# Values one step later, the closing steps reordered, and spare matmuls in TensorE's gaps, in a decode kernel that streams its caches

## The chip, the cores and the metric

One core of a Trainium2 chip. The metric is device microseconds of one execution. The times below are from executions in the fast state, timed in rounds beside the kernel before on the same chip; only the single look at the kernel before (the last row of the table of experiments) has an unknown state. A profiled execution also has a span, from the first to the last instruction; it is some 1.8 us shorter than the device time (211.0 and 212.79 us for the changed kernel). In this kernel TensorE multiplies matrices into tiles of the memory PSUM, VectorE and ScalarE work on them, and DMA engines move the loads (87.32 MB, 87.17 of them through one queue). The views of the profile call TensorE PE (its loading of weights PEld), VectorE DVE, ScalarE ACT and GpSimd POOL.

## The reference, cut to what matters

A decode step of batch 4 with one new token: the sum of the input, an attention branch and an MLP branch. Only the last W = 2048 positions of the caches are read. The arrays are bfloat16.

```python
q = (xn @ wq)                                   # 32 query heads, 16 K/V heads, Dh = 128
scores = einsum(q, k_cache[:, :, -2048:]) * Dh ** -0.5
o = einsum(softmax(scores), v_cache[:, :, -2048:]) @ wo
h = gelu(layernorm(x1) @ w3) @ w4               # 576 -> 4608 -> 576
out = x + o + (x1 + h)
```

With one token, the shifted parts of the MLP's first half are zeros and drop out. What is left is reading 87 MB: 16 K tiles and 16 V tiles of 2 MB each, wq, wo, w3 and w4.

## The kernel before

One queue issues all loads. K and V tiles share a ring of six buffers; the seventh tile waits until the first has been used. The weights w4 come last, in six pieces, so that little work is left when the last bytes land.

```python
    W4_PIECES = [0, NFH, NF - 12, NF - 6, NF - 2, NF - 1, NF]      # rows 0-18-24-30-34-35-36
    order = [("K", 0), ("K", 1), ("K", 2)]
    for h in range(Hkv):
        order.append(("V", h))
        if h + 3 < Hkv:
            order.append(("K", h + 3))
    # ... w3 after V2, wo in four parts ahead of V0, V4, V8, V12, w4 at the end
```

A step t computes the scores of head t, the softmax of head t-1, the values of head t-2 and the output of head t-3. Each step has four slices.

```python
    for t in range(Hkv):
        hm, hv, hf, hp = t - 1, t - 2, t - 3, t - 4
        for s in range(NSL):
            # ... K transpose of the next slice on VectorE; softmax pieces of head hm
            if hv >= 0:
                pv(hv, s)            # O += P^T V, 4 matmuls
            k_scores(t, s)           # 4 matmuls of 512 columns
            # ... output of head hf: o_scale (ScalarE), o_turn (TensorE), o_sum (VectorE)
```

Then come the closing steps.

```python
    sm_max(hl); sm_rec(hl - 1); o_scale(hl - 2)          # hl = 15
    pv(hl - 1, 0); sm_maxT(hl); sm_neg(hl); pv(hl - 1, 1)
    sm_sub(hl); sm_exp(hl); o_turn(hl - 2)
    pv(hl - 1, 2); pv(hl - 1, 3); o_sum(hl - 2)
    sm_turn(hl); sm_den(hl); sm_rec(hl); o_scale(hl - 1)
    for s in range(NSL):
        pv(hl, s)
    o_scale(hl); o_turn(hl - 1); o_sum(hl - 1)
    o_turn(hl); o_sum(hl); o_spread(hl); o_pick(hl)
    mlp_out(*pieces[0])              # 18 rows of w4, sums in acc and acc_odd in turn
    o_proj(hl)                       # the last 16 matmuls with wo
    mlp_out(*pieces[1])
    mlp_out(*pieces[2])
    mlp_out(*pieces[3])
    # ... copy acc_odd to SBUF (ScalarE), pieces 4 and 5 into acc, one add (VectorE), store
```

(Several statements are put on a line here; the kernel has one on each.)

## Time and profile before

| | before |
|---|---|
| device time, median of 3 (range) | 211.53 us (211.49 to 211.63) |
| span of the profiled execution | 209.8 us |
| moved by DMA | 87.32 MB, mean 416 GB/s |
| TensorE waiting for V tiles | 37.1 us |
| first matmul of w4's piece 0 | 201.13 us |
| first matmul of piece 3 | 206.04 us |
| start of the last add | 207.26 us |

From the page of the kernel before, the DMA rows of the span in 40 slices (busy share in tenths, then GB/s):

```profile
DMA  7999999999999999999999999999999999999991
GB/s 301 400 412 437 428 428 428 436 422 428 469 408 420 433 428 427 438 431 428 431 437 428 422 425 446 425 425 436 422 436 428 421 435 440 425 425 448 418 402 72
```

The table of windows of the kernel before. Its columns are the stretch and its length in us, the busy time and instruction count of each engine (PE, PEld, DVE, ACT, POOL), the TensorE clock that was granted (1.00 is full), the busy share of the DMA engines and GB/s:

```profile
126.00:170.00 44.00, 37.23 (x231) 15.68 (x230) 34.02 (x54) 6.88 (x15) 0.00 (x0) 0.96 1.01 431
206.00:206.50 0.50, 0.46 (x8) 0.37 (x8) 0.00 (x0) 0.00 (x0) 0.00 (x0) 1.00 0.26 90
206.50:207.00 0.50, 0.50 (x8) 0.26 (x3) 0.00 (x0) 0.26 (x1) 0.00 (x0) 1.00 0.00 0
```

The loads run without a hole from the first slices to 206.5 us, so they bound this kernel. The mean of 126 to 170 us is 431 GB/s. (Single slices read above that, up to 469, so only the longer means are used here.)

The waits of TensorE for tiles in the kernel before, and VectorE's for K (total us, times, longest us):

```profile
PE O L390 <- DMA vn<-in_A_v_cache_dram: 37.1, 10, 14.0
PE S L338 <- DVE kt L225: 3.1, 1, 3.1
DVE kt L225 <- DMA kn<-in_A_k_cache_dram: 10.6, 1, 10.6
```

TensorE waits for values ten times: compute is ahead of the loads. The end of its timeline before (start, length, engine, line, operation, how many, and in brackets the idle time before it with what ended it), single lines of it:

```profile
201.13 0.29 PE L183 MATMUL acc<-w_sb,gT 128*8 128x288 bf16 x1
205.66 0.29 PE L183 MATMUL acc<-w_sb,gT 128*8 128x288 bf16 x1
206.04 0.28 PE L183 MATMUL acc<-w_sb,gT 128*8 128x288 bf16 x1
207.26 0.45 DVE L613 TENSOR_TENSOR fin<-acc,odd 8x288 bf16<-8x288 f32 x1
```

TensorE works from 201.13 to 205.95 without a gap. It begins piece 3 at 206.04, and the chain of waits says that this was the landing of w4. So TensorE arrives just ahead of the last pieces, by 0.1 to 0.3 us.

### The profile page before, as it was taken

What the parts mean: (1) busy time and instruction counts of PE and PEld (TensorE: products, weight loads), DVE (VectorE), ACT (ScalarE), POOL (GpSimd) and SP (SyncE); (2) the same over time, 40 slices, a digit from 0 to 9 for tenths busy, and PEclk for the clock granted to TensorE, in tenths of its full rate; (3) what the DMA queues carried; (4) which work ended last, traced back from release to release, by engine and by line L of the source; (5) the groups of instructions that cost most, each with busy time, mean ns of one, the idle gap of its engine ahead of it and who ended that gap; (6) DMA issues with size and microseconds to landing.
All of it is one profiled execution on the core that took longest, in us unless ns stands there. A gap on an engine that the chain in (4) does not pass through costs nothing.

```text
span 209.8 us, 2403 instructions
## 1 busy us (share of the span) xinstructions
PE 149.9 (71%) x955; PEld 62.8 (30%) x955; DVE 120.4 (57%) x217; ACT 33.9 (16%) x64; POOL 2.8 (1%) x15
## 2 busy tenths in 40 slices
PE   0287496869694009659899599977994926989884
PEld 0133132223231003214364143332532401425362
DVE  3741899584831082816706869995299471771421
ACT  7602201020211000202102121120111110202300
POOL 4010000000000000000000000000000000000000
PEclk9999589696969556958999979997999985969999
DMA  7999999999999999999999999999999999999991
GB/s 301 400 412 437 428 428 428 436 422 428 469 408 420 433 428 427 438 431 428 431 437 428 422 425 446 425 425 436 422 436 428 421 435 440 425 425 448 418 402 72
DMA packets 6659, 87.32 MB, mean 416 GB/s; under 512 B 748, under 2 KB 1016, under 8 KB 1656
## 3 DMA queue, kind: packets, MB, share of 16 engines
q1 hardware_dynamic: 6640, 87.17, 97.5%
q8 instruction: 7, 0.11, 0.2%
q14 instruction: 4, 0.03, 0.0%
q10 hardware_dynamic: 8, 0.00, 0.0%
HBM read 87.17 MB, written 0.00 MB: 415 GB/s over the span
## 4 chain that ended last, share of the span: by engine, by line
DMA 72%; PE 18%; DVE 6%; ACT 1%; issue 1%; SPq 0%; DVEq 0%
DMA vn<-in_A_v_cache_dram 35%; DMA w_sb<-in_B_w_dram 31%; PE S L338 7%; DMA wq_sb<-in_A_wq_dram 6%; DVE kt L225 3%; PE acc L183 2%; PE g_ps L456 2%; PE q_ps L285 2%; PE O L390 2%; PE oT L403 1%; DVE qz L317 1%; PE gT_ps L468 1%; DVE mx L344 1%; PE S L360 1%; ACT q_sb L296 1%
## 5 line engine op out<-in xcount | busy, mean ns | idle before, releaser
L225 DVE STREAM_TRANSPOSE kt<-kn 128x1024 int32<-128x1024 int32 x64 | 76.4, 1217 | 10.9 <-DMA kn<-in_A_k_cache_dram 10.6
L338 PE MATMUL S<-kt,qz 128*128 128x512 bf16 x256 | 79.7, 441 | 3.1 <-DVE kt L225 3.1
L390 PE MATMUL O<-vn,PT 128*32 128x512 bf16 x256 | 27.4, 426 | 38.9 <-DMA vn<-in_A_v_cache_dram 37.1
L338 PEld LDWEIGHTS <-qz 128*128 128x128 bf16 x256 | 21.7, 104 | 41.5 <-issue 25.8
L366 ACT ACTIVATE E<-S 128x512 bf16<-128x512 f32 x16 | 9.5, 597 | 122.6 <-PE S L360 122.6
L390 PEld LDWEIGHTS <-PT 128*32 128x32 bf16 x256 | 7.2, 94 | 47.3 <-issue 30.2
L372 DVE STREAM_TRANSPOSE PT<-E 128x512 bf16<-128x512 bf16 x16 | 11.4, 710 | 14.9 <-ACT E L366 14.9
L356 DVE TENSOR_REDUCE nm<-mg 8x1 bf16<-8x16 f32 x16 | 2.4, 152 | 20.7 <-PE mg L351 20.7
L397 ACT ACTIVATE O_sb<-O,rd 128x512 f32<-128x512 f32 x16 | 11.0, 686 | 15.6 <-issue 11.0
L413 DVE TENSOR_REDUCE on<-oT 128x8 bf16<-128x128 f32 x16 | 4.5, 280 | 12.7 <-PE oT L403 12.7
L403 PE MATMUL oT<-ident_w,O_sb 128*128 128x128 f32 x64 | 11.1, 302 | 0.3 <-ACT O_sb L397 0.3
L344 DVE TENSOR_REDUCE mx<-S 128x1 f32<-128x512 f32 x16 | 10.5, 657 | 1.3 <-PE S L338 1.3
L403 PEld LDWEIGHTS oT<-ident_w,O_sb 128*128 128x128 f32 x64 | 9.2, 161 | 5.3 <-issue 2.9
L183 PE MATMUL acc<-wo_sb,op 128*8 128x288 bf16 x56 | 7.5, 286 | 0.0
L376 PEld LDWEIGHTS dn<-rs,same_j 128*128 128x128 f32 x32 | 5.8, 188 | 2.9 <-ACT E L366 0.7
L360 PE MATMUL S<-nm,j_row 8*128 8x512 bf16 x16 | 6.5, 409 | 0.0
L329 PE MATMUL S<-negbig,ohT 4*128 4x512 bf16 x16 | 6.2, 385 | 0.0
L351 PE MATMUL mg<-dm,sel_jb 128*8 128x16 bf16 x16 | 2.8, 175 | 3.7 <-DVE dm L346 3.5
L183 PEld LDWEIGHTS <-op 128*8 128x8 bf16 x64 | 4.7, 87 | 2.2 <-issue 0.5
L351 PEld LDWEIGHTS <-sel_jb 128*8 128x8 bf16 x16 | 1.3, 83 | 13.1 <-DVE dm L346 6.5
L183 PE MATMUL acc<-w_sb,gT 128*8 128x288 bf16 x38 | 5.2, 286 | 0.1
L474 DVE COPY g_x<-gT_ps 128x64 f32<-128x64 f32 (+1 forms) x3 | 0.6, 195 | 7.7 <-PE gT_ps L468 7.7
(93 smaller groups left out, 84.3 us busy)
## 6 DMA issues: line engine op xcount, KB each, us to landing
kn<-in_A_k_cache_dram SPq DMA_DIRECT2D x16, 2048.0 KB, 21.9
vn<-in_A_v_cache_dram SPq DMA_DIRECT2D x16, 2048.0 KB, 24.4
wo_sb<-in_A_wo_dram SPq DMA_DIRECT2D x4, 1152.0 KB, 24.5
w_sb<-in_B_w_dram SPq DMA_DIRECT2D x1, 4608.0 KB, 34.3
wq_sb<-in_A_wq_dram SPq DMA_DIRECT2D x1, 4096.0 KB, 12.8
w_sb<-in_B_w_dram SPq DMA_DIRECT2D x1, 2592.0 KB, 31.9
w_sb<-in_B_w_dram SPq DMA_DIRECT2D x2, 864.0 KB, 33.9
w_sb<-in_B_w_dram SPq DMA_DIRECT2D x2, 576.0 KB, 33.0
```

What stands on the lines that cost most here:

```text
L183: nc.tensor.matmul(out=to[q:q + OR, :], lhsT=lhsT[:, NI - 1 - i:NI - 1 - i + OR], rhs=rhs[:, i * CW:(i + 1) * CW], start=start, stop=False ...
L225: nc.vector.transpose(out=kt[:], in_=src)
L329: nc.tensor.matmul(out=S_ps[h][:].rearrange("p (c k) -> p c k", k=QD), lhsT=ohT[:], rhs=negbig[:].unsqueeze(1).to_broadcast([B, SC, QD]), ...
L338: nc.tensor.matmul(out=S_ps[h][:], lhsT=qz[:, z0:z0 + P], rhs=kt[:, ib, :, e:2 * QD:2].rearrange("p c k -> p (c k)"), start=False, stop=Fa ...
L344: nc.vector.reduce_max(out=mx[:], in_=S_ps[h][:], axis=AX.X)
L360: nc.tensor.matmul(out=S_ps[h][:], lhsT=j_row[:], rhs=st.pop(("nm", h))[:, 0:1].to_broadcast([NJ, NW]), start=False, stop=False, skip_grou ...
L366: nc.scalar.activation(out=E[h][:].rearrange("p c k -> p (c k)"), in_=S_ps.pop(h)[:], func=ACT.Exp, scale=scale, accum_out=rs[:])
L372: nc.vector.transpose(out=PT[h][:], in_=E.pop(h)[:])
L376: nc.tensor.matmul(out=dn[:], lhsT=same_j[:], rhs=st.pop(("rs", h))[:], start=True, stop=True)
L390: nc.tensor.matmul(out=O_ps[h][g * QD:(g + 1) * QD], lhsT=PT[h][:, c, :], rhs=vn[:, :, c, :], start=(s == 0), stop=False, skip_group_check ...
L397: nc.scalar.activation(out=O_sb[h][:], in_=O_ps.pop(h)[:], func=ACT.Copy, scale=st.pop(("rd", h))[:, 0:1])
L403: nc.tensor.transpose(out=oT[:, s, :], in_=o[:, s, :], identity=ident_w[:, s * NJ:s * NJ + P])
```

## The change

The intent: with values three steps behind the scores, a step no longer starts with a wait for the V tile that has only just been asked for, and in the closing less is left to do when V15 lands. The output of head 15 now goes through the projection before piece 0. Where TensorE would stand idle, it multiplies into a spare PSUM tile that nobody reads, in order to hold its clock up (in the kernel before it was 0.50 from 184.76 to 188.17 us, after 3.41 us in which TensorE was busy for 1.86 us). The diff, cut:

```diff
-        E[h] = ptp.tile([P, SC, QD], BF16, tag="e", name="E")
+        E[h] = ptp.tile([P, SC, QD], BF16, tag="e", name="E", bufs=1)
-        PT[h] = ptp.tile([P, SC, QD], BF16, tag="pt", name="PT")
+        PT[h] = ptp.tile([P, SC, QD], BF16, tag="pt", name="PT", bufs=3)
...
-    G_AT = 7
+    G_AT = 9                                    # the step that also runs the MLP's w3
-        hm, hv, hf, hp = t - 1, t - 2, t - 3, t - 4
+        hm, hr, hv, hf, hp = t - 1, t - 2, t - 3, t - 4, t - 5
...
+    def keep_warm(n):
+        if not warm:
+            warm.append(ps_s.tile([P, NW], F32, tag="S", name="warm"))
+        for _ in range(n):
+            nc.tensor.matmul(out=warm[0][0:OR, :], lhsT=ln2T[:, 0, 0:OR], rhs=qz[:, 0:NW], start=True, stop=True)
...                                              # head 15's softmax among the values of head 13
+    for s in range(NSL):
+        pv(hl - 1, s)
+    o_turn(hl - 2)
+    o_sum(hl - 2)
     o_scale(hl - 1)
+    o_turn(hl - 1)
+    o_sum(hl - 1)
+    keep_warm(6)
     for s in range(NSL):
         pv(hl, s)
     o_scale(hl)
-    o_turn(hl - 1)
-    o_sum(hl - 1)
...
+    keep_warm(2)
     o_turn(hl)
     o_sum(hl)
+    keep_warm(2)
     o_spread(hl)
     o_pick(hl)
+    keep_warm(4)
+    o_proj(hl)
+    keep_warm(3)
+    pieces = list(zip(W4_PIECES, W4_PIECES[1:]))
     mlp_out(*pieces[0])
-    o_proj(hl)
     mlp_out(*pieces[1])
+    keep_warm(3)
     mlp_out(*pieces[2])
+    keep_warm(1)
     mlp_out(*pieces[3])
```

The spare matmuls fall in three groups, which the text below calls the six (ahead of the values of head 15), the eight (2, 2 and 4, each behind a step that waits for ScalarE or VectorE) and the seven (3, 3 and 1, around the pieces of w4).

More of the change, by code (lines that the diff above doesn't have):

```diff
@@ L527 @@
                     sm_max(hm)
-                if hv >= 0:
-                    sm_rec(hv)
+                if hr >= 0:
+                    sm_rec(hr)
                 if hp >= 0:
@@ L567 @@
         flush_loads()
+    acc_odd = ps_acc.tile([P, CW], F32, tag="g", name="acc_odd")
+    second += [acc_odd, True]
+    warm = []
+    def keep_warm(n):
[3 more added lines that the diff above has]
+            nc.tensor.matmul(out=warm[0][0:OR, :], lhsT=ln2T[:, 0, 0:OR], rhs=qz[:, 0:NW], start=True, stop=True)
     hl = Hkv - 1
@@ L571 @@
     sm_rec(hl - 1)
-    o_scale(hl - 2)
-    pv(hl - 1, 0)
+    o_pick(hl - 4)
+    o_scale(hl - 3)
+    pv(hl - 2, 0)
     sm_maxT(hl)
     sm_neg(hl)
-    pv(hl - 1, 1)
+    pv(hl - 2, 1)
+    o_turn(hl - 3)
     sm_sub(hl)
     sm_exp(hl)
-    o_turn(hl - 2)
-    pv(hl - 1, 2)
-    pv(hl - 1, 3)
-    o_sum(hl - 2)
+    pv(hl - 2, 2)
+    pv(hl - 2, 3)
+    o_sum(hl - 3)
     sm_turn(hl)
+    o_proj(hl - 4)
     sm_den(hl)
     sm_rec(hl)
+    o_scale(hl - 2)
+    for s in range(NSL):
+        pv(hl - 1, s)
+    o_turn(hl - 2)
+    o_sum(hl - 2)
     o_scale(hl - 1)
+    o_turn(hl - 1)
+    o_sum(hl - 1)
+    keep_warm(6)
     for s in range(NSL):
@@ L589 @@
     o_scale(hl)
-    o_turn(hl - 1)
-    o_sum(hl - 1)
-    pieces = list(zip(W4_PIECES, W4_PIECES[1:]))
-    acc_odd = ps_acc.tile([P, CW], F32, tag="g", name="acc_odd")
-    second += [acc_odd, True]
+    keep_warm(2)
     o_turn(hl)
     o_sum(hl)
+    keep_warm(2)
     o_spread(hl)
     o_pick(hl)
+    keep_warm(4)
+    o_proj(hl)
+    keep_warm(3)
+    pieces = list(zip(W4_PIECES, W4_PIECES[1:]))
     mlp_out(*pieces[0])
-    o_proj(hl)
     mlp_out(*pieces[1])
+    keep_warm(3)
     mlp_out(*pieces[2])
+    keep_warm(1)
     mlp_out(*pieces[3])
```

## The prediction

> **What bounds it now.** Loads. The table of windows shows 426 to 432 GB/s and a DMA share of 0.99 to 1.01 in every stretch from 6 to 190 us: the loads never starve. 87.3 MB at about 430 GB/s is 203 us of the 209.8 us span. [...] The chain of waits gives 72% to DMA; TensorE waits 37.1 us for values. Compute is ahead: a step costs TensorE and VectorE 8 to 9 us, a K and V pair about 9.7 us of DMA.
>
> **The end, before** (timeline). Piece 0 of w4 lands at about 200.5 us (168.6 + 31.9). TensorE runs without a gap from 201.13 (piece 0, attention projection, pieces 1, 2) to 205.67, then waits 0.29 us for piece 3, landed at 206.00. The last piece lands at about 206.8 (issue 184.6 + 22.2). Then 0.4 us ACT copy, 0.14 + 0.45 us DVE, store. TensorE already waits for DMA at the end.
>
> **What the change does.**
> - Values one step later. V was loaded right after the K of its step and stalled TensorE at each step's start; now the step waits for K only. The waits move to the K transposes on DVE; nothing is removed.
> - A value buffer is freed one step later, so V(h) is issued with K(h+3), not a step earlier. By my estimate from landing times, 9 to 14 us of loads are still queued then, even in the MLP step (about 4 us longer). No starvation expected. Buffers of wo and w3 also come free later, still ahead of need.
> - Closing: less attention work remains when V15 lands (estimate 194.3 us: V13 at 184.65 and 4.8 us per tile). Traced durations: PV 1.05, scale 0.7, turn 0.66, sum 0.3, spread 0.35, pick 0.85, projection 0.95, gaps: done at about 199.5, before piece 0 lands. TensorE gains some 1.5 to 2 us of slack.
> - 21 spare matmuls of 512 columns, about 0.22 us each at the granted clock of 1.00 after 190 us (four scores take 1.07 us with weight loads): 4.6 us. Six stand before V15, eight in waits on ACT/DVE; the other seven eat the slack. Piece 2 then runs to about 205.7, before piece 3 lands. [...] this trace has the clock at 1.00 in every window from 190 us on: nothing to win.
>
> **On the critical path:** nothing up to piece 3's landing; after it the same few matmuls, copy, add and store. The gain is at most 0.3 us; the loss as small, unless the spare matmuls run slow.
>
> **Predicted:** 211.4 us, 8 in 10 between 210.7 and 212.1. Faster by over 2%: 0.01; within 2%: 0.98; slower by over 2%: 0.01.
>
> **What would show it.** DMA as full as before, 415 GB/s overall; last piece of w4 landing within 0.5 us of 206.8; TensorE's waits for vn nearly gone, DVE's for kn grown to 30 us or more; the last V tiles issued about 10 us later; TensorE idle (or in spare matmuls) before pieces 0 to 3; clock 1.0 at the end, same distance from last landing to end.
>
> **What would make it wrong.** A bubble in the loads after the w3 load or the MLP step, because value buffers come free late (up to a few us); spare matmuls at half clock delaying piece 3 (up to 1 us); the last w4 packets spread differently over the 16 engines (in the last 1.5 us only part of them works), 0.3 us either way.

## The result

| | before | after |
|---|---|---|
| device time, median of 6 (range) | 211.59 us (211.49 to 211.89) | 212.96 us (212.68 to 213.23) |
| ratio, 95% interval | | 1.0062 (1.0048 to 1.0075) |
| span of the profiled execution | 209.8 us | 211.0 us |
| start of the last add | 207.26 us | 208.43 us |

A ratio is the mean time of one kernel's fast runs over that of the other's in the same rounds, so it is not quite the ratio of the medians quoted beside it. The change costs 1.3 us. That is within 2%, but outside the range predicted. The last add starts 1.17 us later, which is the whole difference of the spans.

The same rows of the page after, and the same windows with two more at the end:

```profile
DMA  7999999999998999999999999999999999999990
GB/s 299 398 432 432 429 419 435 430 425 438 489 419 380 445 422 408 449 432 429 432 429 435 425 421 436 441 421 432 436 422 425 430 436 444 404 441 441 404 370 18
```

```profile
126.00:170.00 44.00, 36.41 (x219) 15.66 (x215) 31.56 (x53) 6.78 (x15) 0.00 (x0) 0.92 1.01 431
206.00:206.50 0.50, 0.50 (x9) 0.26 (x6) 0.00 (x0) 0.00 (x0) 0.00 (x0) 1.00 0.21 74
206.50:207.00 0.50, 0.50 (x11) 0.35 (x7) 0.00 (x0) 0.00 (x0) 0.00 (x0) 1.00 0.00 0
207.00:207.50 0.50, 0.50 (x10) 0.29 (x6) 0.00 (x0) 0.00 (x0) 0.00 (x0) 1.00 0.00 0
207.50:208.00 0.50, 0.50 (x8) 0.36 (x5) 0.00 (x0) 0.07 (x1) 0.00 (x0) 1.00 0.00 0
```

The loads are as full as before and end in the same window, 206.0 to 206.5. No time was lost there, although buffers come free a step later. The difference is that TensorE is now still busy after them: in 207.0 to 208.0 it has 1.00 us of work. The waits of TensorE after, and the wait of VectorE to which those for values have moved:

```profile
PE S L338 <- DVE kt L225: 31.3, 10, 14.3
```

```profile
DVE kt L225 <- DMA kn<-in_A_k_cache_dram: 36.7, 10, 15.0
```

There is no wait for V any more. As predicted, the waiting has moved from V to K: TensorE's waits for V go from 37.1 us to none, its waits for K's transposes from 3.1 us to 31.3, and VectorE's waits for K itself from 10.6 us to 36.7. In sum none of it is gone: TensorE was idle for 59.9 us of the span before; after, it was idle for 56.7 us and in spare matmuls for about 4.5 us (21 of 0.215; the six of them at 195.43 us took 1.29 us). The end of the timeline after, single lines of it:

```profile
192.96 1.05 PE L390 MATMUL O<-vn,PT 128*32 128x512 bf16 x16
194.85 0.66 PE L403 MATMUL oT<-ident_w,O_sb 128*128 128x128 f32 x4 [0.26 <-ACT O_sb L397]
195.43 1.03 PE L577 MATMUL warm<-qz,ln2T 128*8 128x512 bf16 x4
196.53 1.23 PE L390 MATMUL O<-vn,PT 128*32 128x512 bf16 x10
197.59 0.59 PE L577 MATMUL warm<-qz,ln2T 128*8 128x512 bf16 x2
201.06 0.29 PE L183 MATMUL acc<-wo_sb,op 128*8 128x288 bf16 x1
202.26 0.38 PE L577 MATMUL warm<-qz,ln2T 128*8 128x512 bf16 x1
202.47 0.38 PE L577 MATMUL warm<-qz,ln2T 128*8 128x512 bf16 x1
208.43 0.43 DVE L635 TENSOR_TENSOR fin<-acc,odd 8x288 bf16<-8x288 f32 x1
```

From 201.06 on, not one gap of TensorE is left: it never waits for w4. A spare matmul shows as 0.38 us long, but the next starts 0.21 us after it (202.26, 202.47), and that spacing is what it costs. The values of head 15 are held behind the six, and piece 3 is begun at 207.2 us, when the loads have ended.

### The profile page after: what moved, and what is told of

Its sections match the earlier page's. It is cut to its first block, busy times and chain, and to the rows that moved or that the text cites. A ratio compares the mean times of both kernels' runs of the same rounds, so it can differ in the third digit from the quotient of the medians.

```text
span 211.0 us, 2418 instructions
## 1 busy us (share of the span) xinstructions
PE 154.3 (73%) x976; PEld 64.6 (31%) x976; DVE 120.2 (57%) x217; ACT 33.8 (16%) x64; POOL 2.7 (1%) x15
## 4 chain that ended last, share of the span: by engine, by line
DMA 63%; PE 24%; DVE 5%; issue 3%; SPq 2%; ACT 1%; DVEq 0%; ACTq 0%
DMA kn<-in_A_k_cache_dram 63%; PE S L338 8%; PE acc L183 4%; PE O L390 4%; DVE kt L225 3%; PE oT L403 2%; PE g_ps L456 2%; PE warm L577 2%; DVE mx L344 1%; SPq L103 1%; PE S L360 1%; ACT O_sb L397 1%; PE gT_ps L468 1%; DVE dm L346 1%; PE mg L351 0%
## 5 line engine op out<-in xcount | busy, mean ns | idle before, releaser
L338 PE MATMUL S<-kt,qz 128*128 128x512 bf16 x256 | 78.8, 437 | 31.4 <-DVE kt L225 31.3
L225 DVE STREAM_TRANSPOSE kt<-kn 128x1024 int32<-128x1024 int32 x64 | 76.6, 1222 | 37.0 <-DMA kn<-in_A_k_cache_dram 36.7
L338 PEld LDWEIGHTS <-qz 128*128 128x128 bf16 x256 | 22.6, 104 | 69.6 <-issue 53.5
L403 PE MATMUL oT<-ident_w,O_sb 128*128 128x128 f32 x64 | 12.0, 320 | 0.7 <-ACT O_sb L397 0.7
L360 PE MATMUL S<-nm,j_row 8*128 8x512 bf16 x16 | 7.0, 439 | 0.1
L183 PE MATMUL acc<-wo_sb,op 128*8 128x288 bf16 x48 | 6.5, 286 | 0.0
L577 PE MATMUL warm<-qz,ln2T 128*8 128x512 bf16 x21 | 5.7, 379 | 0.0
L183 PE MATMUL acc_odd<-w_sb,gT 128*8 128x288 bf16 x34 | 5.3, 286 | 0.0
L285 PE MATMUL q_ps<-wq_sb,xnT 128*32 128x512 bf16 x40 | 4.1, 594 | 0.9 <-DMA wq_sb<-in_A_wq_dram 0.9
```

Source lines behind the costliest of these rows:

```text
L183: nc.tensor.matmul(out=to[q:q + OR, :], lhsT=lhsT[:, NI - 1 - i:NI - 1 - i + OR], rhs=rhs[:, i * CW:(i + 1) * CW], start=start, stop=False ...
L225: nc.vector.transpose(out=kt[:], in_=src)
L338: nc.tensor.matmul(out=S_ps[h][:], lhsT=qz[:, z0:z0 + P], rhs=kt[:, ib, :, e:2 * QD:2].rearrange("p c k -> p (c k)"), start=False, stop=Fa ...
L360: nc.tensor.matmul(out=S_ps[h][:], lhsT=j_row[:], rhs=st.pop(("nm", h))[:, 0:1].to_broadcast([NJ, NW]), start=False, stop=False, skip_grou ...
L403: nc.tensor.transpose(out=oT[:, s, :], in_=o[:, s, :], identity=ident_w[:, s * NJ:s * NJ + P])
L577: nc.tensor.matmul(out=warm[0][0:OR, :], lhsT=ln2T[:, 0, 0:OR], rhs=qz[:, 0:NW], start=True, stop=True)
```

## The experiments

The theory after reading the two traces: spare matmuls are paid for at 0.215 us each wherever ready work stands behind them, and the thirteen that stand so cost more than the slack there is. The rivals: the shift of the values or the new order costs the time (later buffers, later closing); or the spare matmuls are needed to hold the clock, and without them the loss would be larger. The "expected" texts call the theory A, later A/D, the rivals B and C, and the theory on the wait for K15 (below) E. The table gives all twelve runs; "over before" is against the kernel before.

| run | median us | before | ratio to before (95%) |
|---|---|---|---|
| no spare matmul | 211.95 | 211.66 | 1.0012 (0.9995 to 1.0029) |
| without the six | 212.04 | 211.66 | 1.0014 (0.9998 to 1.0030) |
| without the seven | 211.98 | 211.66 | 1.0010 (0.9996 to 1.0024) |
| without the eight | 213.46 | 211.66 | 1.0082 (1.0067 to 1.0098) |
| changed kernel again | 213.48 | 211.73 | 1.0064 (1.0040 to 1.0089) |
| only the eight | 211.72 | 211.73 | 0.9995 (0.9976 to 1.0014) |
| before, plus seven | 211.75 | 211.73 | 1.0007 (0.9981 to 1.0034) |
| seven doubled | 214.72 | 211.73 | 1.0130 (1.0108 to 1.0153) |
| changed, plus 14 at K15 | 212.16 | 211.57 | 1.0025 (1.0011 to 1.0039) |
| only the eight, plus 14 at K15 | 211.75 | 211.57 | 1.0008 (0.9994 to 1.0023) |
| before, plus fourteen | 212.88 | 211.57 | 1.0060 (1.0045 to 1.0075) |
| before again, one look | 211.50 | 211.57 | not timed in rounds |

All twelve gave correct results.

### All spare matmuls out

```diff
-    keep_warm(6)
...                  # and every other keep_warm
-    keep_warm(1)
```

> The changed kernel with all 21 spare matmuls taken out and nothing else. Theory A (spare matmuls stand in TensorE's serial path after V15 and use up more than the 1.2 us of slack there): the last add starts at about 207.3 us again, as before the change; ratio to before 0.999 to 1.001, about 211.6 us; TensorE waits again for piece 3 at about 206.0. Theory B (values one step later, or the reordering itself, cost the time): stays at about 1.006. Theory C (the spare matmuls hold the clock up): slower than the changed kernel, and a granted clock below 1 after 194 us.

Measured: 1.0012, back at the kernel before within the interval. So the spare matmuls cost the time, and the shift and the order together cost at most 0.3% (the end of the interval); each of the two alone was not run. But theory C's mechanism is in the trace as well. The table of windows of this run, cut where the clock changes (at 200.0 and 203.4 us) and one window of the same length earlier:

```profile
196.60:200.00 3.40, 1.47 (x24) 0.73 (x12) 0.93 (x3) 0.69 (x1) 0.00 (x0) 1.00 0.97 413
200.00:203.40 3.40, 3.13 (x28) 1.75 (x30) 0.21 (x1) 0.00 (x0) 0.00 (x0) 0.50 1.00 415
```

In 196.6 to 200.0 TensorE was busy 1.47 of 3.40 us, and in the next 3.4 us the clock was 0.50. The last projection ran in that stretch at 0.24 us for two matmuls in place of 0.12. The stretch at 0.50 is 3.4 us long and begins 17.0 us, five times that length, after the one before it (183.0 us). TensorE was not idle in the window ahead of it. In this run TensorE met no wait for w4 and the last add began at 207.65, 0.39 us later than before: the slowed clock used up the slack that leaving out the spare matmuls gave and, in this profile, a little more. My expectation that TensorE would wait for piece 3 at 206.0 did not hold here.

### One group out at a time

```diff
-    keep_warm(6)                               # "without the six"
```

> Only the six spare matmuls ahead of the values of head 15 are taken out. Theory A: they took 1.29 us (195.43 to 196.72) ahead of PV15, all later work moves up by that, and the loads then bound the end: 1.17 us or a little less is won, ratio to before 1.000 to 1.001. Theory B or C: within 0.2 us of the changed kernel, 1.005 to 1.007. If TensorE was waiting for V15 there anyway: also no gain.

```diff
     o_proj(hl)                                 # "without the seven"
-    keep_warm(3)
...
-    keep_warm(3)
     mlp_out(*pieces[2])
-    keep_warm(1)
```

> Only the seven between the last projection and piece 3 (3, 3 and 1) are taken out. Theory A: 7 x 0.215 = 1.5 us less on TensorE's path, the loads bound the end: ratio to before 0.999 to 1.001, not additive with the six. Theory B or C: 1.005 to 1.007.

```diff
     o_scale(hl)                                # "without the eight"
-    keep_warm(2)
...
-    keep_warm(2)
...
-    keep_warm(4)
```

> Only the eight that stand in waits for ScalarE and VectorE (2, 2 and 4) are taken out. Theory A: they fill real waits, so almost nothing is won, 0 to 0.2 us: ratio to before 1.005 to 1.007. If every spare matmul costs its time wherever it stands (8 x 0.215 = 1.7 us): ratio 1.000. Theory C: slower than the changed kernel.

Measured: 1.0014, 1.0010 and 1.0082. Leaving out the six wins nearly everything, and so does leaving out the seven, so the two gains cannot add up. The expected reason, that the loads take over as the bound, is not in these two traces: in neither does TensorE wait for w4, and the last add begins at 207.70 and 207.77, still 0.4 to 0.5 us later than before. It is in the trace with both out (next section). Leaving out the eight wins nothing; the point estimate is even above the expected 1.005 to 1.007, but not apart from the changed kernel's own 1.0064 (1.0040 to 1.0089). It was run on another chip. Spare matmuls of 0.215 us each cost about 1 us for six or nothing for eight, by where they stand. That refutes both "each one costs" and "the shift costs the loss".

The changed kernel without the six and with them: from the transposes of head 14's output to the two spare matmuls behind head 15's values it is 195.40 to 196.86 without, 194.85 to 197.59 with. The difference is 1.28 us for six.

### Only the eight, beside the changed kernel itself

```diff
-    keep_warm(6)
...
-    keep_warm(3)
...
-    keep_warm(3)
     mlp_out(*pieces[2])
-    keep_warm(1)
```

> The changed kernel once more, unedited, as the control on this chip. Every theory: ratio to before 1.005 to 1.009, about 1.2 to 1.9 us over.

> The changed kernel with only the eight spare matmuls kept that stand in waits for ScalarE and VectorE; the six and the seven are out. Theory D (position decides: what stands in a wait is free and keeps the clock at 1.00, what stands between ready work costs 0.215 us each): the granted clock is 1.00 from 194 us to the end, unlike without any spare matmul, where it fell to 0.75; the last projection starts at about 200.3, pieces 0 to 2 are done before piece 3 lands, TensorE waits for the load; ratio to before 0.998 to 1.001, no slower than without any. If the shift or the reordering cost time of their own: 1.001 to 1.004.

Measured: the control 1.0064, only the eight 0.9995. The last stretches of the run with only the eight, windows and then single lines of the timeline:

```profile
194.00:198.00 4.00, 3.32 (x39) 1.59 (x29) 0.58 (x2) 1.38 (x2) 0.00 (x0) 1.00 1.00 430
198.00:202.00 4.00, 3.98 (x48) 2.18 (x48) 1.14 (x3) 0.00 (x0) 0.00 (x0) 1.00 0.94 389
```

```profile
193.39 1.05 PE L390 MATMUL O<-vn,PT 128*32 128x512 bf16 x16
200.21 0.29 PE L183 MATMUL acc<-wo_sb,op 128*8 128x288 bf16 x1
205.24 0.28 PE L183 MATMUL acc<-w_sb,gT 128*8 128x288 bf16 x1 [0.94 <-DMA w_sb<-in_B_w_dram]
206.62 0.28 PE L183 MATMUL acc<-w_sb,gT 128*8 128x288 bf16 x1 [0.48 <-DMA w_sb<-in_B_w_dram]
207.84 0.45 DVE L631 TENSOR_TENSOR fin<-acc,odd 8x288 bf16<-8x288 f32 x1
```

The same of the control (head 14's values and the last add), and of the run without the seven (the last projection and the last add):

```profile
193.88 1.05 PE L390 MATMUL O<-vn,PT 128*32 128x512 bf16 x16
209.35 0.43 DVE L635 TENSOR_TENSOR fin<-acc,odd 8x288 bf16<-8x288 f32 x1
```

```profile
201.91 0.29 PE L183 MATMUL acc<-wo_sb,op 128*8 128x288 bf16 x1
207.77 0.43 DVE L632 TENSOR_TENSOR fin<-acc,odd 8x288 bf16<-8x288 f32 x1
```

The clock stays at 1.00 (in every window from 190 to 207 us), and TensorE again waits for w4: 0.94 us ahead of piece 2 and 0.48 us ahead of piece 3. That is the slack of the new order. The two brackets understate it, because they count from the end of a matmul that overlaps the next (0.29 us long, with two begun every 0.12 us). From the last projection to the last add it is 7.63 us here and 5.86 in the run without the seven, which has the same work there and no wait: the loads held TensorE up by 1.77 us. (This profile is of the slowest of the six executions, 212.20 us: it began piece 3 at 206.62 us, 0.58 later than before. With loads as early as before, the slack would be about 1.2 us by this estimate.) That closes the account of the loss between the two traces. The thirteen are 2.80 us, which exceeds 1.77 by 1.03; the control also began head 14's values 0.49 us later. The sum is 1.52 us; the control's last add is 1.51 us later. In time, the run with only the eight and the run with none are not apart: their intervals overlap. What the eight do is shown by the clock rows only.

### The seven doubled

```diff
     o_proj(hl)
-    keep_warm(3)
+    keep_warm(6)
...
-    keep_warm(3)
+    keep_warm(6)
     mlp_out(*pieces[2])
-    keep_warm(1)
+    keep_warm(2)
```

> The changed kernel with the seven doubled to fourteen (6, 6 and 2 in place of 3, 3 and 1). Theory A/D: TensorE bounds the end already, so all of 7 x 0.215 = 1.5 us is added: 1.4 to 1.6 us over the changed kernel of the same call. If there were slack left to eat: less than 1 us.

Measured: 1.0130 against the control's 1.0064, 1.4 us for seven more. From the start of head 14's values to the last add it is 16.98 us (193.47 to 210.45), in the control 15.47 us (193.88 to 209.35): 1.51 us, as worked out. TensorE bounds the end of the changed kernel.

### Spare matmuls in the kernel before

```diff
+    keep_warm(3)
     mlp_out(*pieces[0])
     o_proj(hl)
     mlp_out(*pieces[1])
+    keep_warm(3)
     mlp_out(*pieces[2])
+    keep_warm(1)
     mlp_out(*pieces[3])
```

> The kernel before, old order and values two steps behind, with only seven spare matmuls added: three ahead of piece 0, three ahead of piece 2, one ahead of piece 3. Theory A/D: 7 x 0.215 = 1.5 us on TensorE's path less the 0.3 us that it waited for piece 3: 1.2 us slower, ratio 1.005 to 1.0065. If only the new order makes TensorE late: ratio below 1.002.

Measured: 1.0007. This was a miss: I expected 1.2 us and got nothing that can be told from zero. The trace says why. In the profile of before, which gave the 0.3 us of slack, the clock was at half during step 15; in the profile of this run it was not. Windows of before, then of this run:

```profile
184.00:186.00 2.00, 1.35 (x7) 0.39 (x7) 1.93 (x6) 0.00 (x0) 0.00 (x0) 0.69 1.03 442
186.00:188.00 2.00, 2.00 (x10) 0.44 (x9) 1.24 (x3) 0.00 (x0) 0.00 (x0) 0.50 1.07 459
```

```profile
184.00:186.00 2.00, 1.39 (x13) 0.46 (x12) 1.93 (x6) 0.00 (x0) 0.00 (x0) 1.00 1.07 459
186.00:188.00 2.00, 2.00 (x17) 1.05 (x17) 2.00 (x4) 0.00 (x0) 0.00 (x0) 1.00 1.03 442
```

The start of head 15's values, in before and then here:

```profile
197.92 1.05 PE L390 MATMUL O<-vn,PT 128*32 128x512 bf16 x16
```

```profile
196.39 1.05 PE L390 MATMUL O<-vn,PT 128*32 128x512 bf16 x16
```

They began at 196.39 us here and at 197.92 in before, so 1.5 us more slack was there to eat. The slack of the old order was 0.3 us in one profile and about 1.8 (0.3 and 1.5) in the other. Of this run's six times, two were 212.57 and 213.06 against 211.5 to 211.8 of the rest. An execution with the smaller slack would look like that, but those two left no profile, and three of the eleven times of the unedited kernel in the same call were 212.43 to 212.53 as well, so nothing is shown by them. I then doubled the addition, to see whether that is the limit, and took one more profile of the kernel before:

```diff
-    keep_warm(3)
+    keep_warm(6)
     mlp_out(*pieces[0])
...
-    keep_warm(3)
+    keep_warm(6)
     mlp_out(*pieces[2])
-    keep_warm(1)
+    keep_warm(2)
```

> The kernel before with fourteen in place of the seven that cost it nothing measurable (6 ahead of piece 0, 6 ahead of piece 2, 2 ahead of piece 3), 3.0 us. If the old order has about 1.7 us of slack, as the trace with seven shows when no half-clock window falls on step 15: 1.2 to 1.5 us slower than before, ratio 1.005 to 1.008. With 0.3 us of slack, as the profile of before shows with such a window: 2.7 us, 1.012. If spare matmuls cost nothing in the old order at all: below 1.002.

> The kernel before, unedited, one more profile. If the place of the half-clock windows varies from execution to execution: the window at 184.8 to 188.2 us of the first profile lies elsewhere or is missing, and TensorE begins piece 0 at 199.5 to 200.5 and waits for loads by over 1 us, with the same total. If not: the same window, piece 0 begun at about 201.1.

Measured: fourteen cost 1.3 us (1.0060). Fourteen are 3.0 us, so 1.7 us of them was absorbed, close to what the trace with seven had said. The old order is no exception to the rule. The second profile of before had its half-clock window where the first had it (0.65 in 184 to 186, 0.50 in 186 to 188), with piece 0 begun at 200.98. So the two profiles of the unedited kernel have the window and the two of the edited ones don't, although the edits come later in the program. The traces show how busy TensorE was ahead of it. In the first profiles of before and after, every stretch between two changes of the clock is a whole multiple of 3.41 us (the longest 30.72); for the other three profiles used here I laid the same grid through their own changes. The window of that grid with TensorE's gap in step 15 was busy for 1.86 us in the first profile of before (181.35 to 184.76) and 1.88 in the second (181.17 to 184.59), and half clock (0.50) followed; it was busy for 2.26 us with the seven (182.33 to 185.74) and 2.40 with the fourteen (182.62 to 186.03), and full clock (1.00) followed. The grid lies about 1 us later in the edited ones. Whether that is chance or the edit, four profiles cannot say.

### The wait for K15

In the eight profiles of the new order without a filling there, TensorE waits 2.1 to 4.9 us for K15's first transpose, and a stretch at half clock (0.50) falls into step 15. In the changed kernel, windows cut where the clock changes:

```profile
178.00:181.40 3.40, 0.41 (x2) 0.19 (x2) 1.71 (x2) 0.00 (x0) 0.00 (x0) 1.00 1.03 434
181.40:184.80 3.40, 2.99 (x12) 0.70 (x11) 3.36 (x7) 0.00 (x0) 0.00 (x0) 0.50 1.00 429
```

If this delays the closing, filling that wait should help even a kernel that suffers from too many spare matmuls.

```diff
                 pv(hv, s)
+            if t == Hkv - 1 and s == 0:
+                fill15 = ps_acc.tile([P, NW], F32, tag="g", name="fill15")
+                for _ in range(14):
+                    nc.tensor.matmul(out=fill15[0:OR, :], lhsT=ln2T[:, 0, 0:OR], rhs=qz[:, 0:NW],
+                                     start=True, stop=True)
             k_scores(t, s)
```

> The changed kernel, all 21 spare matmuls kept, plus 14 more where TensorE waits for K15 (ahead of the first scores of head 15, 3.3 us idle in the changed kernel's trace). Theory E (that idle time halves the clock in the next window, near 181 to 187, which makes head 15's chain and so the whole closing late): the half-clock window there goes, the values of head 14 start 0.8 to 1.4 us earlier than in the control (193.88), and as TensorE bounds the end the total falls by 0.8 to 1.3 us: ratio to before 1.000 to 1.003. If the clock there does not matter: 1.005 to 1.008. If spare matmuls always cost: slower still, 1.01 or more.

> As the run with only the eight kept, plus the 14 in the wait for K15: the version with the most slack on TensorE. Theory D/E: TensorE waits for the w4 pieces by 2 us or more in all, but the loads bound the end, so no gain over the kernel before: ratio 0.998 to 1.001. A gain of over 0.3 us would say that something other than the loads bounds the end of the kernel before.

Measured: the changed kernel with fourteen more spare matmuls is faster, 1.0025 in place of 1.0064. Its clock and its values of head 14:

```profile
182.00:184.00 2.00, 1.10 (x9) 0.41 (x9) 1.96 (x5) 0.00 (x0) 0.00 (x0) 1.00 0.98 418
```

```profile
176.04 3.19 PE L550 MATMUL fill<-qz,ln2T 128*8 128x512 bf16 x14
...
192.22 1.05 PE L390 MATMUL O<-vn,PT 128*32 128x512 bf16 x16
```

The half-clock stretch is gone and head 14's values start at 192.22, where the control had 193.88 and the first profile of the changed kernel 192.96. 1.0025 and 1.0064 are of two chips. The second run joins this with the best of the others: the clock is 1.00 in every window from 176 to 208 us, and TensorE waits 1.5 us for w4 by the brackets (2 us or more had been expected). It gave 1.0008 (0.9994 to 1.0023): no gain over before, as expected where the loads bound the end. No version that I ran beats the kernel before.

## Why the prediction was wrong

Right: the loads bound the kernel before; they stay full with buffers freed a step later (431 GB/s in 126 to 170 us in both); the waits for V move to K (TensorE's for V 37.1 us to none, VectorE's for K 10.6 to 36.7); the last bytes land where they did; a spare matmul costs 0.22 us (0.215); there was nothing for the clock to win at the end of the old order. A small miss beside these: the last V tiles were issued 4.9 us later (163.62 in place of 158.72 for the first of the last three), not about 10.

Wrong: the step "Closing: ... done at about 199.5, before piece 0 lands. TensorE gains some 1.5 to 2 us of slack", and with it "Six stand before V15 ... the other seven eat the slack". Two terms of that sum were mis-sized.

1. I started head 15's values when V15 lands, at an estimated 194.3 us. The landing does not bound them: in no profile of the new order does TensorE wait for V15. Its own queue does. Head 15's softmax and head 14's values stand in front, after a wait for K15 that half clock follows (0.50 from 181.4 to 184.8 us in the changed kernel; 1.00 with the wait filled). Without the six, head 15's values began at 195.99 us; in the profile of the changed kernel itself the queue reached the six at 195.43. With the wait for K15 filled, head 14's values came 1.66 us earlier than in the control, 0.74 earlier than in the first profile.
2. I counted the six as free, as if they stood in a wait for V15. They stand behind work that is ready and ahead of work that is ready, and cost 1.28 us.

So the last projection began at 201.06 and not at about 198.5 (199.5 less its own 0.95): 1.13 us of that from the queue (195.43 in place of 194.3) and 1.28 from the six. The chain behind head 15's values was rightly sized: 4.34 us to the projection without the six (195.99 to 200.33), 4.25 in my sum. And the seven (1.5 us, rightly sized) met a slack of 1.2 to 1.8 us that the six (1.28) had already used up, wholly or for the most part. The prediction named as a danger that spare matmuls run at half clock. They ran at full clock (1.00 from 190 to 208 us in the changed kernel); there were simply too many in places where nothing was waited for. The range of 210.7 to 212.1 covered a loss of 0.6 us at most, and the loss was 1.3.

What stays open: what sets where the clock's grid lies, and with it whether the half-clock window falls on step 15 of the old order, and so how the old order's slack, 0.3 or 1.7 us, is spread over executions. The shift of the values and the new order were only run together.

## What to carry to other kernels

In these runs a spare matmul cost nothing that shows where TensorE waited for another engine or a load (only the eight: 0.9995), and its full 0.215 us was on the path where the next instruction was ready (1.28 us for the six, 1.51 us for seven more in the changed kernel); put it behind the instruction whose result is waited for, and count the wait before choosing the number. In these traces TensorE worked in order, and the arrival of the last tile was not the start of its work, because the queue in front of it was not empty by then (estimated landing 194.3 us, reached by the queue at 195.43): add up the queue, not the landing times. Where the loads bound the end, look at how far ahead of the last pieces TensorE arrives: that slack is all that an addition may take (of fourteen, 3.0 us, the old order absorbed 1.7), and here a reordering that made it larger gained nothing by itself (0.9995 and 1.0008 over before).

## What the runs show of the clock and of spare matmuls

- With no spare matmuls the clock went to 0.50 after a window with 1.47 of 3.40 us busy, in which no single wait of TensorE was longer than 1.0 us. Without the eight, windows with 2.47 and 2.12 of 3.40 us busy (196.8 to 203.6 us) were not followed by a lower clock (1.00 in every window from 190 us on). These are single windows; how busy one must be was not shown. (A matmul's end is modelled, so the busy times are rough.)
- Of the matmuls issued only to hold the clock, thirteen in the wrong places cost 1.3 us net, eight in waits cost nothing that shows, and fourteen in the wait for K15 won about 0.8 us in the changed kernel (1.0064 to 1.0025 over before, in two calls) and nothing in the version that the loads bound (1.0008).
